# One-bank PSUM tiles throughout, a 384/128 split of the last tile, and newly made orders in a fused attention and GeGLU kernel

## The chip, the cores and the metric

The kernel runs on one NeuronCore of one Trainium2 chip. The metric is the device time in microseconds (us) of one launch. Before the change it is 216.15 us, the median of three runs (215.91 to 216.42).

## What is computed

The input is x, 2048 rows (tokens) of 512 in bf16. It is normalised once, and two branches use the result xn. Branch A is attention over a sliding, dilated window; branch B is a gated feed-forward net. The output is x + A * silu(B).

```python
xn = layernorm(x)
q, k, v = heads(xn @ wqkv)              # 32 heads of 16
# token s looks at s, s-2, ..., s-14 (8 places, those below 0 masked)
logits = einsum("hsd,hswd->hsw", q, k_window) * 16**-0.5
o = einsum("hsw,hswd->hsd", softmax(logits), v_window)
A = o @ wo
h = gelu(xn @ w_gate) * (xn @ w_up)     # 512 -> 1792
B = h @ w_down                          # 1792 -> 512
out = x + A * silu(B)
```

## The kernel before, in words

**Blocks and tiles.** The 2048 tokens are four blocks j = 0 to 3 of 512 tokens, and a block is four tiles tt of 128. For each block TensorE (PE) computes, with matmuls that are nearly all 128x128 by 128x512:

- q, k, v (`qkv`, L527; block 0 tile by tile with 128 columns, L611),
- the gate and up halves of the feed-forward net (`ffn`, L907): 14 chunks fc of each, four matmuls a chunk, named g and u with block and chunk, such as g1_2,
- the down projection (`down`, L971), named y with block, tile, piece and quarter: y0_1_0_2 is block 0, tile 1, piece 0, third quarter. A tile takes 14 matmuls in quarters of 4, 4, 4 and 2,
- the output projection (`out`, L1035), named s: four matmuls a tile.

**Evacuation.** ScalarE (ACT) empties nearly all PSUM tiles: gelu (L923), plain copies of u (L931) and of q, k, v (L542, L544, L549), silu of y (L990), a copy of s (L1050). VectorE (DVE) multiplies gelu and u into h (`geglu`, L945), which the down projection reads. DVE also has the attention: products q*k (L704) and their sums (L716, L720), the softmax, products with v (L850) and their sums.

**The logit sums.** A logit is a sum over 16 products that lie on different partitions. Blocks 1 to 3 form it with accumulating DMAs on GpSimd's queue (`gathered`, L780). Block 0 (`psum=(0,)`) does it on PE (`reduced`): eight matmuls with a matrix of ones (L740) fill a PSUM tile `L0` of two banks; DVE then adds the mask at the sequence's start (L747), takes the maximum over the 8 places (`peak`, L750) and subtracts it (`less`, L757). ACT takes the exponential (L811).

**PSUM.** Eight banks of 128x512 f32 are divided in `POOLS`: pool F has six one-bank tiles, and pool L one tile of two banks. Pool L is for `L0` and, with `shared=True`, for the tiles 0 and 1 of every block's y: `ps_y{j}` of shape [128, 2, 512] holds tile 0 in its first bank and tile 1 in its second. All else goes through F. Dependences are kept by tile: an instruction that writes a tile is made to wait for those that read the same tile earlier in the program's order, whichever bank they read.

**The order of the work.** A planner (`schedule`, L125) walks through all operations with estimated durations, priorities and the list `nudge` of one correction for each operation, and gives one fixed order for each engine and one fixed bank (slot of a pool) for each PSUM tile. The engines then run these orders, each in sequence, with semaphore waits; a waiting instruction holds up all that stands behind it on its engine. The estimates and nudges decide the order only; they are no part of the program.

**The end.** In block 3 the last tile (tt = 3) is split by columns in two pieces at `CUT` = 256, in `down` and in `out`, so that its first piece can be finished and stored while PE still works on the second. The pieces' s is multiplied from PSUM by silu(y) on DVE (gate, L1090), x is added (L1096), and a DMA stores it (L1102); SyncE issues the first piece's store, ACT the second's.

**ACT's tables.** ACT holds one table set at a time. Sqrt (L318), gelu, exp and silu lie in different sets, so each switch inserts a table load; copies need none.

Of the kernel before, what the change touches and what calls it, by code (L numbers as in the profile page):

```python
# [10 lines left out]
ALU = mybir.AluOpType  # L11
AF = mybir.ActivationFunctionType
AX = mybir.AxisListType
BF16 = mybir.dt.bfloat16
F32 = mybir.dt.float32

P = 128
H = 32
DH = 16
W = 8  # L20
# [7 lines left out]
CUT = 256  # L28
# [27 lines left out]
POOLS = {"F": 6, "L": 1, "q": 2, "k": 2, "pr": 5, "attn": 2, "Ls": 1, "v": 2, "o": 1, "oT": 1, "h": 1,  # L56
# [3 lines left out]
    sums=(3,), warm=4, slack=4.68, N=[298.0, 85.4, 406.1, 719.1], psum=(0,), shared=True, rpow=False,  # L60
    S=[238.4, -534.3, 59.4, -251.7], V=[-282.7, -31.0, 282.4, -70.3], Q=[42.0, -337.6, 71.1, 38.0],
    F=[33.6, 79.9, 263.9, 443.0], Y=[-104.4, 20.0, -67.6, -114.6], O=[15.4, -370.2, -327.0, 457.0], vnorm=(),
    vcopy=(1,), vsum=(0,), crowd=1.35,
    nudge=[
# [162 lines left out]
class Kernel:  # L227
# [11 lines left out]
    def new(self, key, shape, dtype, name):  # L239
        pool, slot = self.pool_of[key], self.slot[key]  # L240
        space = self.ps if pool in ("F", "L") else self.sb
        self.t[key] = space.tile(shape, dtype, name=name, tag=f"{pool}{slot}")
        return self.t[key]
# [37 lines left out]
    def layernorm(self, j):  # L281
        base = self.when("N", j)
        for tt in range(TPB):
# [94 lines left out]
            if by_act:  # L378
# [13 lines left out]
                self.op(f"mean{t}", "ACT", 0.62, [f"ld_x{j}_{j}"], mean, prio=prio, slack=(0.0, 0.5, 3.0, 3.0)[j])  # L392
                self.op(f"aggr{t}", "ACT", 0.70, [f"mean{t}"], square, prio=prio)
# [338 lines left out]
    def reduced(self, j):  # L732


        def reduce():
            L = self.new(f"L{j}", [P, 2, TQ], F32, "L_ps")
            for w2 in range(2):
                for tq in range(TPB):
                    pr = self.t[f"pr{j}_{tq // 2}_0"][:, 0, tq % 2, 4 * w2 : 4 * w2 + 4]
                    self.nc.tensor.matmul(  # L740
                        L[H * tq : H * (tq + 1), w2, :], lhsT=self.ind[:],
                        rhs=pr.rearrange("p w t -> p (w t)"), start=True, stop=True,
                    )

        def masked():
            first = self.t["L0"][0:H, :, :].rearrange("p a (b t) -> p (a b) t", b=4)[:, :, 0:PAD]
            self.nc.vector.tensor_tensor(out=first, in0=first, in1=self.mask[:], op=ALU.add)  # L747

        def peak():
            self.nc.vector.tensor_reduce(  # L750
                out=self.peak[:], in_=self.t[f"L{j}"][:].rearrange("p a (b t) -> p t (a b)", b=4),
                axis=AX.X, op=ALU.max,
            )

        def less():
            ls = self.new(f"Ls{j}", [P, W, P], F32, "Ls")
            self.nc.vector.tensor_tensor(  # L757
                out=ls[:], in0=self.t[f"L{j}"][:].rearrange("p a (b t) -> p (a b) t", b=4),
                in1=self.peak[:].unsqueeze(1).to_broadcast([P, W, P]), op=ALU.subtract,
            )  # L760
# [4 lines left out]
        if j == 0:  # L765
            self.op("mask0", "DVE", 0.2, ["red0"], masked, use=["L0"], prio=hot)
# [524 lines left out]
```

## Time and profile before

| what | value |
|---|---|
| median of three runs | 216.15 us |
| the profiled execution: its own time | 215.84 us |
| its span (first to last recorded instruction) | 214.1 us |
| granted TensorE clock | 0.999 of full speed |
| PE, ACT, DVE, GpSimd (POOL) busy | 206.4, 153.1, 187.1, 65.6 us |
| matmul records, ACT table loads | 1105, 19 |

In the rows, the first number is the start in us from the span's start or, in grouped rows, the count after an x. PE is the matmul stream and PEld the loads of weights that run beside it, one for each matmul. A matmul record has a modelled end: a 512-column matmul is shown with 379 ns, though the next starts 0.216 us after it. So the spacing of starts, best read from the weight loads, tells the rate. "[1.45 <-ACT sil L990]" at the end of a row is idle time of the engine before it, and what ended it. In a row of windows the busy time of each engine follows its name.

### The profile page before, as it was taken

To read this page: it belongs to the slowest core of one execution; us is meant where nothing else is said; L and a number is where in the kernel's file an instruction comes from. 1 tells how busy PE (TensorE), PEld (TensorE's weight loads), DVE (VectorE), ACT (ScalarE), POOL (GpSimd) and SP (SyncE) were. 2 spreads that over 40 slices of the span, in tenths; PEclk is the share of its full clock that TensorE was granted. 3 is DMA by queue.
4 is the path that set the end of the run, shared out by engine and by line. 5 is a ranking of instruction groups with operands and counts; after the bars stand their busy time and mean duration, and the time that the engine had idled before them with its cause. 6 is when DMAs were issued, how large, how long until landed. Compare 5 with 4: busy or idle time off the path is not lost.

```text
span 214.1 us, 3070 instructions
## 1 busy us (share of the span) xinstructions
PE 206.4 (96%) x1105; PEld 102.4 (48%) x1123; DVE 187.1 (87%) x211; ACT 153.1 (71%) x258; POOL 65.6 (31%) x108
## 2 busy tenths in 40 slices
PE   7999999999997999999999999999999999999993
PEld 2896444444443444444444544444444444445452
DVE  4698998499899996999999999999999989997114
ACT  3687699999997998767943767877341689665442
POOL 5043200001226679140367740279701010101000
PEclk9999999999999999999999999999999999999999
DMA  5999997205246678762697886168958069506902
GB/s 192 362 382 375 287 278 202 54 0 98 79 117 127 130 135 155 153 167 44 102 168 106 158 212 140 49 116 169 171 99 196 0 132 232 126 2 130 253 13 98
DMA packets 32991, 32.17 MB, mean 150 GB/s; under 512 B 16960, under 2 KB 29520, under 8 KB 32976
## 3 DMA queue, kind: packets, MB, share of 16 engines
q0 software_dynamic: 5136, 14.41, 35.2%
q1 hardware_dynamic: 27008, 16.91, 28.9%
q10 hardware_dynamic: 832, 0.66, 0.9%
q8 instruction: 9, 0.15, 0.3%
q14 instruction: 6, 0.05, 0.1%
HBM read 14.12 MB, written 6.31 MB: 95 GB/s over the span
## 4 chain that ended last, share of the span: by engine, by line
PE 81%; DVE 10%; ACT 6%; issue 2%; ACTq 0%; DVEq 0%
PE u_ps L907 20%; PE y_ps L971 20%; PE g_ps L907 19%; PE qkv_ps L527 14%; PE s_ps L1035 5%; DVE prod L704 4%; PE warm_ps L253 2%; DVE prod L716 2%; PE qkv_ps L611 1%; DVE stats L290 1%; DVE s L1090 1%; DVE s L1096 1%; ACT gl L923 1%; ACT L923 1%; ACT L318 1%
## 5 line engine op out<-in xcount | busy, mean ns | idle before, releaser
L907 PE MATMUL g_ps<-xnT,wg_sb 128*128 128x512 bf16 x219 | 53.5, 379 | 0.3
L971 PE MATMUL y_ps<-wd_sb,hT 128*128 128x512 bf16 (+1 forms) x233 | 51.7, 366 | 2.0 <-ACT sil L990 1.7
L907 PE MATMUL u_ps<-xnT,wu_sb 128*128 128x512 bf16 x221 | 52.9, 379 | 0.2
L780 POOL DMA_DIRECT2D Ls<-prod x48 | 36.4, 887 | 29.0 <-DMA Ls<-prod 10.6
L923 ACT ACTIVATE gl<-g_ps 128x512 bf16<-128x512 f32 x56 | 31.9, 596 | 17.7 <-PE g_ps L907 16.3
L704 DVE TENSOR_TENSOR prod<-q_sb,k_sb 128x2048 bf16<-128x2048 bf16 x32 | 38.0, 1217 | 2.9 <-ACT k_sb L544 1.7
L931 ACT ACTIVATE hT<-u_ps 128x512 bf16<-128x512 f32 x56 | 32.3, 599 | 10.3 <-PE u_ps L907 7.7
L971 PEld LDWEIGHTS <-hT 128*128 128x128 bf16 x238 | 23.3, 98 | 27.5 <-issue 2.4
L850 DVE TENSOR_TENSOR pv<-attn,v_arr 128x4096 bf16<-128x4096 bf16 x16 | 36.2, 2285 | 0.2
L907 PEld LDWEIGHTS <-wu_sb 128*128 128x128 bf16 x224 | 21.9, 98 | 26.4
L907 PEld LDWEIGHTS <-wg_sb 128*128 128x128 bf16 x224 | 21.8, 98 | 26.3 <-issue 0.4
L945 DVE TENSOR_TENSOR hT<-hT,gl 128x1024 bf16<-128x1024 bf16 x28 | 18.8, 681 | 3.1 <-ACT gl L923 2.3
L716 DVE TENSOR_TENSOR prod<-prod 128x2048 bf16<-128x2048 bf16 x16 | 19.1, 1216 | 0.1
L873 POOL DMA_DIRECT2D pv<-pv x4 | 3.5, 886 | 40.1 <-DVE pv L850 40.1
L1035 PE MATMUL s_ps<-wo_sb,oT_sb 128*128 128x512 bf16 (+1 forms) x67 | 15.2, 366 | 0.1
L857 DVE TENSOR_TENSOR pv<-pv 128x2048 bf16<-128x2048 bf16 x12 | 14.4, 1217 | 0.1
L676 POOL DMA_DIRECT2D v_arr<-vT_dram x16 | 10.8, 717 | 11.4 <-DMA vT_dram<-vst 5.9
L990 ACT ACTIVATE sil<-y_ps 128x512 bf16<-128x512 f32 (+1 forms) x17 | 9.1, 575 | 6.6 <-PE y_ps L971 6.6
L1050 ACT ACTIVATE s<-s_ps 128x512 bf16<-128x512 f32 x15 | 9.0, 600 | 5.8 <-PE s_ps L1035 5.6
L569 POOL DMA_DIRECT2D vT_dram<-vst x12 | 7.9, 658 | 15.5 <-ACT vst L549 15.5
L527 PE MATMUL qkv_ps<-xnT,wv_sb 128*128 128x512 bf16 x47 | 11.9, 379 | 0.1
L527 PE MATMUL qkv_ps<-xnT,wk_sb 128*128 128x512 bf16 x48 | 11.8, 379 | 0.0
(93 smaller groups left out, 224.9 us busy)
## 6 DMA issues: line engine op xcount, KB each, us to landing
Ls<-prod POOLq DMA_DIRECT2D x48, 128.0 KB, 3.7
v_arr<-vT_dram POOLq DMA_DIRECT2D x16, 142.0 KB, 4.6
vT_dram<-vst POOLq DMA_DIRECT2D x16, 128.0 KB, 3.5
pv<-pv POOLq DMA_DIRECT2D x4, 512.0 KB, 4.5
oT_dram<-o_sb SPq DMA_DIRECT2D x16, 128.0 KB, 3.3
oT_sb<-oT_dram SPq DMA_DIRECT2D x4, 512.0 KB, 4.3
wg_sb<-in_B_w_gate_dram SPq DMA_DIRECT2D x2, 896.0 KB, 10.1
wu_sb<-in_B_w_up_dram SPq DMA_DIRECT2D x2, 896.0 KB, 12.4
```

What stands on the lines that cost most here:

```text
L527: self.nc.tensor.matmul(ps[:], lhsT=self.w_qkv(which, dk, c), rhs=self.t[f"xT{j}"][:, dk, :], start=(dk == 0), stop=(dk == NC - 1),)
L704: self.nc.vector.tensor_tensor(out=self.t[pair][:, c % 2].rearrange("p n w t -> p w n t"), in0=q.unsqueeze(1).to_broadcast([P, W, 2, P]), ...
L716: self.nc.vector.tensor_tensor(out=pr[:, 0], in0=pr[:, 0], in1=pr[:, 1], op=ALU.add)
L780: self.nc.gpsimd.dma_start(out=self.t[f"Ls{j}"][H * tq : H * (tq + 1)], in_=self.t[f"pr{j}_{tq // 2}_0"][s::NC, 0, tq % 2], **(dict(accum_ ...
L850: self.nc.vector.tensor_tensor(out=pv[:], in0=self.t[f"at{j}"][:, 2 * i : 2 * i + 2, :].unsqueeze(2).to_broadcast([P, 2, DH, P]), in1=win, ...
L857: self.nc.vector.tensor_tensor(out=pv[:, 0], in0=pv[:, 0], in1=pv[:, 1], op=ALU.add)
L907: nc.tensor.matmul(ps[:], lhsT=w[:, dk, fc * P : (fc + 1) * P], rhs=self.t[f"xT{j}"][:, dk, :], start=(dk == 0), stop=(dk == NC - 1),)
L923: self.nc.scalar.activation(out=self.t[f"gl{j}_{pair}"][:, fc % 2, :], in_=self.t[f"ps_g{j}_{fc}"][:], func=AF.Gelu_apprx_tanh,)
L931: self.nc.scalar.activation(out=self.t[f"h{j}"][:, fc, :], in_=self.t[f"ps_u{j}_{fc}"][:], func=AF.Copy)
L945: self.nc.vector.tensor_tensor(out=h, in0=h, in1=self.t[f"gl{j}_{pair}"][:], op=ALU.mult)
L971: nc.tensor.matmul(self.t["ps_" + key][:, 0 : n1 - n0], lhsT=self.t[f"h{j}"][:, fc, tt * P : (tt + 1) * P], rhs=self.wd_sb[:, fc, n0:n1], ...
L1035: self.nc.tensor.matmul(ps[:, 0 : n1 - n0], lhsT=self.t[f"oT{j}"][:, c, tt * P : (tt + 1) * P], rhs=self.wo_sb[:, c, n0:n1], start=(c == 0 ...
```

## The change

1. `POOLS`: pool F has eight one-bank tiles, pool L is gone, and so is `shared`. Each y tile has a bank of its own.
2. `reduced`: block 0's logit sums go into two one-bank tiles of F. What DVE does with them is done in halves: two mask additions, two maxima and one maximum of the two (into a new small tile `peak2`), and two subtractions.
3. `CUT` is 384: the last tile's pieces are 384 and 128 columns wide, in y and in s.
4. Orders: `nudge`, the priorities (N, S, V, Q, F, Y, O), `slack` and the planner's estimates for two ACT operations (`mean`, `aggr`) are other numbers. All engines' orders are new. ACT has 23 table loads where it had 19: one more pair (sqrt, then gelu again) stands early in block 0's feed-forward net, and one more pair (gelu, then silu again) between block 1's silus. Both programs have 2248 PE instructions; those of the kinds above are the same but for the pieces' widths.

```diff
-CUT = 256
+CUT = 384
...
-POOLS = {"F": 6, "L": 1, "q": 2, "k": 2, "pr": 5, "attn": 2, "Ls": 1, "v": 2, "o": 1, "oT": 1, "h": 1,
+POOLS = {"F": 8, "q": 2, "k": 2, "pr": 5, "attn": 2, "Ls": 1, "v": 2, "o": 1, "oT": 1, "h": 1,
...
         def reduce():
-            L = self.new(f"L{j}", [P, 2, TQ], F32, "L_ps")
             for w2 in range(2):
+                L = self.new(f"L{j}_{w2}", [P, TQ], F32, "L_ps")
                 for tq in range(TPB):
...
-        def masked():
-            first = self.t["L0"][0:H, :, :].rearrange("p a (b t) -> p (a b) t", b=4)[:, :, 0:PAD]
-            self.nc.vector.tensor_tensor(out=first, in0=first, in1=self.mask[:], op=ALU.add)
+        def masked(w2):
+            first = view(w2)[0:H, :, 0:PAD]
+            self.nc.vector.tensor_tensor(
+                out=first, in0=first, in1=self.mask[:, half * w2 : half * (w2 + 1), :], op=ALU.add
+            )
...
+        def both():
+            self.nc.vector.tensor_tensor(out=self.peak[:], in0=self.peak[:], in1=self.peak2[:], op=ALU.max)
...
+        for w2 in range(2):
+            before = self.op(f"peak{j}_{w2}", "DVE", 0.66, [before], lambda w2=w2: peak(w2), use=banks, prio=hot)
+        before = self.op(f"peak{j}", "DVE", 0.2, [before], both, prio=hot)
+        for w2 in range(2):
+            before = self.op(f"less{j}" + "a" * (1 - w2), "DVE", 0.62, [before], lambda w2=w2: less(w2),
...
-                        if a == 0 and (tt > 1 or not self.par["shared"]):
-                            self.t["ps_" + key] = self.new("ps_" + key, [P, D], F32, "y_ps")[:]
-                        elif a == 0:
-                            if tt == 0:
-                                self.new(f"ps_y{j}", [P, 2, D], F32, "y_ps")
-                            self.t["ps_" + key] = self.t[f"ps_y{j}"][:, tt, :]
+                        if a == 0:
+                            self.new("ps_" + key, [P, D], F32, "y_ps")
...
-                                 take=[("FL"[both], bank)] if a == 0 and not (both and tt) else [],
+                                 take=[("F", bank)] if a == 0 else [],
```

The new order of PE around the end of block 0's down projection, which the prediction speaks of:

```
before: ... y0_0_0_3 y0_1_0_2 y0_1_0_3 y0_3_0_2 y0_3_0_3 u1_4 k2_3 v2_3 q2_0 v2_1 ...
after:  ... y0_0_0_3 y0_1_0_2 y0_1_0_3 y0_3_0_3 u1_4 u1_0 y0_2_0_3 g1_4 v2_3 v2_1 ...
```

At the end PE's order is now s3_0 s3_2 s3_1, then the last six matmuls of y's 384-column piece and its s3_3_0, then ten matmuls of y's 128-column piece and the four of s3_3_1. Before, it was s3_0 s3_3_0 s3_2 s3_1, then ten matmuls of y's second piece and s3_3_1.

More of the change, by code (lines that the diff above doesn't have):

```diff
@@ L54 @@
 WORK = {"turn": 0.8, "st": 0.42, "ld": 0.82, "sto": 0.6, "ldo": 1.8, "acc": 2.6, "gat": 0.45, "out": 0.8, "end": 0.05}
-POOLS = {"F": 6, "L": 1, "q": 2, "k": 2, "pr": 5, "attn": 2, "Ls": 1, "v": 2, "o": 1, "oT": 1, "h": 1,
+POOLS = {"F": 8, "q": 2, "k": 2, "pr": 5, "attn": 2, "Ls": 1, "v": 2, "o": 1, "oT": 1, "h": 1,
          "xT": 2, "gl": 3, "sil": 1, "s16": 1, "xn": 4, "vst": 4}
 PARAMS = dict(
-    sums=(3,), warm=4, slack=4.68, N=[298.0, 85.4, 406.1, 719.1], psum=(0,), shared=True, rpow=False,
-    S=[238.4, -534.3, 59.4, -251.7], V=[-282.7, -31.0, 282.4, -70.3], Q=[42.0, -337.6, 71.1, 38.0],
-    F=[33.6, 79.9, 263.9, 443.0], Y=[-104.4, 20.0, -67.6, -114.6], O=[15.4, -370.2, -327.0, 457.0], vnorm=(),
+    sums=(3,), warm=4, slack=2.82, N=[306.5, 111.8, 418.2, 728.4], psum=(0,), rpow=False,
+    S=[237.0, -554.0, 60.7, -257.2], V=[-277.9, -35.1, 276.7, -102.3], Q=[43.7, -338.2, 71.3, 36.8],
+    F=[34.7, 79.8, 266.5, 442.4], Y=[-106.0, 20.0, -72.7, -105.7], O=[19.3, -380.8, -324.0, 455.3], vnorm=(),
     vcopy=(1,), vsum=(0,), crowd=1.35,
     nudge=[
[43 rows of a table removed]
[44 rows of a table added]
     ],
@@ L240, in new @@
         pool, slot = self.pool_of[key], self.slot[key]
-        space = self.ps if pool in ("F", "L") else self.sb
+        space = self.ps if pool == "F" else self.sb
         self.t[key] = space.tile(shape, dtype, name=name, tag=f"{pool}{slot}")
@@ L390, in square @@
                     )
-                self.op(f"mean{t}", "ACT", 0.62, [f"ld_x{j}_{j}"], mean, prio=prio, slack=(0.0, 0.5, 3.0, 3.0)[j])
-                self.op(f"aggr{t}", "ACT", 0.70, [f"mean{t}"], square, prio=prio)
+                self.op(f"mean{t}", "ACT", 0.70, [f"ld_x{j}_{j}"], mean, prio=prio, slack=(0.0, 0.5, 3.0, 3.0)[j])
+                self.op(f"aggr{t}", "ACT", 0.75, [f"mean{t}"], square, prio=prio)
             elif t == 1:
@@ L732, in reduced @@
     def reduced(self, j):
+        half = W // 2
         def reduce():
-            L = self.new(f"L{j}", [P, 2, TQ], F32, "L_ps")
             for w2 in range(2):
+                L = self.new(f"L{j}_{w2}", [P, TQ], F32, "L_ps")
                 for tq in range(TPB):
-                    pr = self.t[f"pr{j}_{tq // 2}_0"][:, 0, tq % 2, 4 * w2 : 4 * w2 + 4]
+                    pr = self.t[f"pr{j}_{tq // 2}_0"][:, 0, tq % 2, half * w2 : half * (w2 + 1)]
                     self.nc.tensor.matmul(
-                        L[H * tq : H * (tq + 1), w2, :], lhsT=self.ind[:],
+                        L[H * tq : H * (tq + 1), :], lhsT=self.ind[:],
@@ L742, in reduce, with view @@
                         rhs=pr.rearrange("p w t -> p (w t)"), start=True, stop=True,
                     )
-        def masked():
-            first = self.t["L0"][0:H, :, :].rearrange("p a (b t) -> p (a b) t", b=4)[:, :, 0:PAD]
-            self.nc.vector.tensor_tensor(out=first, in0=first, in1=self.mask[:], op=ALU.add)
-        def peak():
+        def view(w2):
+            return self.t[f"L{j}_{w2}"][:].rearrange("p (w t) -> p w t", w=half)
+        def masked(w2):
[3 more added lines that the diff above has]
+            )
@@ L750, in peak @@
+        def peak(w2):
             self.nc.vector.tensor_reduce(
-                out=self.peak[:], in_=self.t[f"L{j}"][:].rearrange("p a (b t) -> p t (a b)", b=4),
-                axis=AX.X, op=ALU.max,
-            )
-        def less():
-            ls = self.new(f"Ls{j}", [P, W, P], F32, "Ls")
+                out=(self.peak, self.peak2)[w2][:], in_=view(w2).rearrange("p w t -> p t w"), axis=AX.X, op=ALU.max
+            )
+        def both():
+            self.nc.vector.tensor_tensor(out=self.peak[:], in0=self.peak[:], in1=self.peak2[:], op=ALU.max)
@@ L757, in less @@
+        def less(w2):
+            if w2 == 0:
+                self.new(f"Ls{j}", [P, W, P], F32, "Ls")
             self.nc.vector.tensor_tensor(
-                out=ls[:], in0=self.t[f"L{j}"][:].rearrange("p a (b t) -> p (a b) t", b=4),
-                in1=self.peak[:].unsqueeze(1).to_broadcast([P, W, P]), op=ALU.subtract,
+                out=self.t[f"Ls{j}"][:, half * w2 : half * (w2 + 1), :], in0=view(w2),
+                in1=self.peak[:].unsqueeze(1).to_broadcast([P, half, P]), op=ALU.subtract,
@@ L760, in less @@
             )
         hot = -10.0
-        self.op(f"red{j}", "PE", 2 * MM, [f"ladd{j}_0", f"ladd{j}_1"], reduce, mode="tiled", take=[("L", f"L{j}")],
-                use=[f"pr{j}_0_0", f"pr{j}_1_0", f"L{j}"], prio=-100.0, slack=self.par["slack"])
-        if j == 0:
-            self.op("mask0", "DVE", 0.2, ["red0"], masked, use=["L0"], prio=hot)
-        self.op(f"peak{j}", "DVE", 1.24, [f"red{j}" if j else "mask0"], peak, use=[f"L{j}"], prio=hot)
-        self.op(f"less{j}", "DVE", 1.15, [f"peak{j}"], less, take=[("Ls", f"Ls{j}")], use=[f"L{j}", f"Ls{j}"], prio=hot)
+        banks = [f"L{j}_0", f"L{j}_1"]
@@ new lines, in reduced @@
+        self.op(f"red{j}", "PE", 2 * MM, [f"ladd{j}_0", f"ladd{j}_1"], reduce, mode="tiled",
+                take=[("F", b) for b in banks], use=[f"pr{j}_0_0", f"pr{j}_1_0", *banks], prio=-100.0,
+                slack=self.par["slack"])
+        before = f"red{j}"
+        for w2 in range(2):
+            if j == 0:
+                before = self.op(f"mask0_{w2}", "DVE", 0.15, [before], lambda w2=w2: masked(w2), use=banks, prio=hot)
+        for w2 in range(2):
+            before = self.op(f"peak{j}_{w2}", "DVE", 0.66, [before], lambda w2=w2: peak(w2), use=banks, prio=hot)
@@ L770, in gathered @@
+        before = self.op(f"peak{j}", "DVE", 0.2, [before], both, prio=hot)
+        for w2 in range(2):
+            before = self.op(f"less{j}" + "a" * (1 - w2), "DVE", 0.62, [before], lambda w2=w2: less(w2),
+                             take=[("Ls", f"Ls{j}")] if w2 == 0 else [], use=[*banks, f"Ls{j}"], prio=hot)
     def gathered(self, j):
@@ L977, in down @@
                     need = before + [f"geglu{j}_{p}" for p in range(a // 2, b // 2)] + ["ld_wd" + "a" * (b <= 8)]
-                    both = tt < 2 and self.par["shared"]
-                    if both and tt and a == 0:
-                        need.append(f"mm_y{j}_0_0_0")
-                    bank = f"ps_y{j}" if both else "ps_" + key
+                    bank = "ps_" + key
                     nm = self.op(f"mm_{key}_{i}", "PE", (b - a) * MM * (n1 - n0) / D, need, mms,
-                                 take=[("FL"[both], bank)] if a == 0 and not (both and tt) else [],
+                                 take=[("F", bank)] if a == 0 else [],
                                  use=[bank, f"h{j}"], prio=base + 3.05 * tt + 0.9 * i + si, slack=self.par["slack"])
@@ L1226 @@
     k.peak = cpool.tile([P, P], F32, name="peak")
+    k.peak2 = cpool.tile([P, P], F32, name="peak2")
     k.junk = cpool.tile([P, D], BF16, name="junk")
```

87 rows, old and new, of the table nudge are left out of this document.

## The prediction

> **What bounds the kernel now.** I read the page's head and its chain of waits first, then who waited for whom on PE, then the timeline at each wait.
>
> ```profile
> span 214.1 us, 3070 instructions
> PE 206.4 (96%) x1105; PEld 102.4 (48%) x1123; DVE 187.1 (87%) x211; ACT 153.1 (71%) x258; POOL 65.6 (31%) x108
> PE 81%; DVE 10%; ACT 6%; issue 2%; ACTq 0%; DVEq 0%
> PE y_ps L971 <- ACT sil L990: 1.7, 2, 1.5
> ```
>
> PE is busy 96% of the span, and 81% of the chain that ended last is PE. Once it runs, the longest sum of waits on PE is that of the down projection (L971) for silu on ACT, 1.7 us in two waits. So a microsecond that PE loses in mid-kernel is lost to the end, unless something else is late there too. How long PE really stood is read from the weight loads, whose starts show the rate:
>
> ```profile
> 62.24 3.55 PEld L971 LDWEIGHTS <-hT 128*128 128x128 bf16 x17
> 67.52 1.39 PEld L971 LDWEIGHTS <-hT 128*128 128x128 bf16 x7 [1.73 <-issue]
> 62.45 3.62 PE L971 MATMUL y_ps<-wd_sb,hT 128*128 128x512 bf16 x16
> 67.52 1.89 PE L971 MATMUL y_ps<-wd_sb,hT 128*128 128x512 bf16 x8 [1.45 <-ACT sil L990]
> 66.87 0.60 ACT L990 ACTIVATE sil<-y_ps 128x512 bf16<-128x512 f32 x1
> 126.01 2.26 PEld L971 LDWEIGHTS <-hT 128*128 128x128 bf16 x11
> 128.55 1.82 PEld L971 LDWEIGHTS <-hT 128*128 128x128 bf16 x9 [0.29 <-issue]
> 127.90 1.57 ACT L990 ACTIVATE sil<-y_ps 128x512 bf16<-128x512 f32 x3
> 198.06 4.92 PE L971 MATMUL y_ps<-wd_sb,hT 128*128 128x512 bf16 x25
> 202.58 0.60 ACT L990 ACTIVATE sil<-y_ps 128x512 bf16<-128x512 f32 x1 [2.42 <-PE y_ps L971]
> 203.23 2.97 PE L971 MATMUL y_ps<-wd_sb,hT 128*128 128x512 bf16 x14 [0.25 <-ACT sil L990]
> ```
>
> The records of 16 and of 8 matmuls differ by 8: (3.62 - 1.89)/8 = 0.216 a matmul. The 17th weight load belongs to y0_1_0_2, whose matmul was due at 62.24 + 17 x 0.216 = 65.91. It started at 67.52, right after the silu of y0's tile 0 (66.87 + 0.60): **1.61 us lost**. Tiles 0 and 1 share one two-bank tile, so the write of tile 1 waits for the read of tile 0, though they are in different banks. The same meets y1_1 at 128.55, after silu1_0 ended (127.90 + 0.60 = 128.50): due at 126.01 + 11 x 0.216 = 128.39, **0.16 lost**. And y3_1 at 203.23, after silu3_0 (203.18): its record of 25 ends at 202.98 with a 256-column matmul of 0.27, which gives way after 0.11 (both from the rows of the tail, below), so it was due at 202.82: **0.41 lost**. Together 2.18 us.
>
> **The change part by part.**
>
> *One bank for each y tile.* The three waits have no cause left: tile 1 has its own bank, whose last reader was done before its first quarter. Taken off: 2.18 us. What is late next? PE runs 1.6 us ahead of where it was, so it asks for banks sooner, and ACT has to give them. ACT stands thus:
>
> ```profile
> 18.00:66.00 48.00, 47.74 (x223) 21.99 (x227) 42.57 (x54) 45.03 (x80) 6.70 (x11) 1.00 0.58 151
> 34.00:66.00 32.00, 31.84 (x151) 14.71 (x153) 27.33 (x35) 31.29 (x56) 4.09 (x7) 1.00 0.33 72
> 100.00:130.00 30.00, 29.84 (x137) 14.00 (x138) 29.93 (x28) 18.56 (x31) 16.05 (x22) 1.00 0.85 145
> 18.99 0.24 ACT L586 ACTIVATE k_sb<-k_sb 128x64 bf16<-128x64 bf16 x1
> 19.25 1.28 ACT L923 ACT_TABLE_LOAD   x1
> 20.55 1.08 ACT L923 ACTIVATE gl<-g_ps 128x512 bf16<-128x512 f32 x2
> ```
>
> The columns after the length are PE, PEld, DVE, ACT and POOL. From 18 to 66 us ACT idles 48.00 - 45.03 = 2.97 us, but from 34 on only 0.71. The new order does the same 84 ACT operations ahead of silu0_0, and one sqrt/gelu pair of table loads more, early: 2 x 1.28 = 2.56. If the idle time takes it all, silu0_0 ends where it did, at 67.47; if none, at 70.03. In the new order PE does 0.43 less work ahead of y0_1_0_2 (two matmuls), so it gets there at 65.91 - 0.43 = 65.48. The first group that takes the bank of y0_0 is v2_3, with 22 matmuls between (2 + 2 + 4 + 4 + 2 + 4 and the four of y0_1_0_2): 65.48 + 22 x 0.216 = 70.23. So PE finds this bank free with 0.2 to 2.8 us to spare. Then v2_1, at 71.1, takes y0_1's, whose silu stands two operations further (norm15 0.7 and itself 0.6): 68.8 to 71.3. Even at the bad end PE waits about 0.2. I take 0, since the idle time is over the 2.56, and keep up to 2.56 for later groups.
>
> The Trainium skill, page "ScalarE: Activation LUTs", section "What ACT_TABLE_LOAD costs", prices a switch at 1283 ns for the load and about 1380 ns for a drain. The rows show the load but no drain: one ends at 19.23, the load runs from 19.25, and the next activation starts at 20.55. With the drain four more loads would be 10.6 us of ACT, not 5.1; I hold to the rows.
>
> The second pair stands between silu1_0 and silu1_3, where ACT idles 11.4 us of 30 (the row from 100). I take 0 there too.
>
> *Logit sums in two banks.* PE's eight matmuls are the same. DVE's work is cut up:
>
> ```profile
> L747 DVE TENSOR_TENSOR L_ps<-L_ps,mask 32x128 f32<-32x128 f32 x1 | 0.3, 287 | 0.8 <-PE L_ps L740 0.8
> L750 DVE TENSOR_REDUCE peak<-L_ps 128x128 f32<-128x1024 f32 x1 | 1.2, 1226 | 0.0
> L757 DVE TENSOR_TENSOR Ls<-L_ps,peak 128x1024 f32<-128x1024 f32 x1 | 1.2, 1224 | 0.0
> L817 DVE TENSOR_TENSOR tot<-attn 128x512 f32<-128x512 bf16 x4 | 2.7, 687 | 3.7 <-ACT attn L811 3.7
> 38.24 1.22 DVE L757 TENSOR_TENSOR Ls<-L_ps,peak 128x1024 f32<-128x1024 f32 x1
> 40.35 1.28 ACT L811 ACT_TABLE_LOAD   x1
> 41.64 1.06 ACT L811 ACTIVATE attn<-Ls 128x1024 bf16<-128x1024 f32 x1
> 42.73 0.69 DVE L817 TENSOR_TENSOR tot<-attn 128x512 f32<-128x512 bf16 x1 [2.98 <-ACT attn L811]
> ```
>
> No row has the halves. A half of the maximum or the subtraction lies between 0.61 (half) and 1.22 (no saving); the 512-element row gives 0.69, and I take that. The maximum of two works on 128 elements like the mask row, 0.29. A half mask lies between 0.14 and 0.29; I take 0.22. Sum: 2 x 0.22 + 4 x 0.69 + 0.29 = 3.49 for 2.74, so 0.75 more (0.3 to 3.0 more). The cover: the subtraction ended at 39.46, while ACT's exponential came only at 41.64, behind its table load, and DVE then idled 2.98. Up to 2.2 us are free; without that cover it would be 0.75 of DVE, and geglu behind it. I take 0.
>
> *The 128-column piece.* Its matmuls are shown by block 0's rows of that width:
>
> ```profile
> 7.50 0.61 PE L611 MATMUL qkv_ps<-xnT,wk_sb 128*128 128x128 bf16 x8
> 9.07 1.06 PE L611 MATMUL qkv_ps<-xnT,wk_sb 128*128 128x128 bf16 x16
> 209.06 1.25 PE L971 MATMUL y_ps<-wd_sb,hT 128*128 128x256 bf16 x10
> 210.15 0.60 PE L1035 MATMUL s_ps<-wo_sb,oT_sb 128*128 128x256 bf16 x4
> ```
>
> (1.06 - 0.61)/8 = 0.056 each, against 0.054 for a quarter of 0.216; 256 columns take (1.25 - 0.60)/6 = 0.108, and one such record 0.60 - 3 x 0.108 = 0.27. Eighteen matmuls of 128 columns cost 0.04 more; 384 columns, not shown, lie between 0.108 and 0.216, on the line at 0.162. The Trainium skill, "TensorE: Matmul & The Clock Gate", section "Back-to-back issue gap", gives 81 ns for each 128-column matmul in a sustained stream with its weight loads: a rule against narrow pieces, 18 x 25 ns = 0.45 us by it. The rows of 8 and 16 are such a stream and show 56.
>
> *The tail.*
>
> ```profile
> 210.86 0.42 DVE L1090 TENSOR_TENSOR s<-s_ps,sil 128x256 bf16<-128x256 f32 x1
> 211.32 0.29 DVE L1096 TENSOR_TENSOR s<-s,x_sb 128x256 bf16<-128x256 bf16 x1
> 211.64 0.37 ACTq L1102 DMA_DIRECT2D out_dram<-s  x1
> ```
>
> Now PE's last matmul starts at 210.15 + 3 x 0.108 = 210.47, and the last store is issued at 211.64: 1.17 later. After the change, count from the start S of the last 384-column matmul. Fourteen of 128 columns follow, the last at S + 0.16 + 13 x 0.056 = S + 0.89. DVE's gate of the 384 piece starts at S + 0.38 (matmul 0.33, hand-over 0.05) and takes 0.55 (256 columns take 0.42; 0.42 to 0.84), its addition 0.36 (0.29 to 0.58), the gate of 128 columns 0.28 and its addition 0.22 (each from half of the 256 row to all of it). With 0.04 between dependent ones and 0.08 of overlap between the pieces, the store goes out at about S + 1.82, or 0.93 after PE's last start. That last start is 0.05 later against the same total of columns, since the final matmul is the shorter one. Saved: 1.17 - 0.93 - 0.05 = 0.19 (0.4 lost to 0.4 gained). The landing (211.64 to 214.1) I leave.
>
> **The sum**, against the profiled execution's own 215.84 us: -2.18 + 0.04 - 0.19 = -2.33, so 213.5. The median shown, 216.15, is 0.31 higher; I forecast the median: **213.8 us**, with 213.2 to 214.6 for this case by itself.
>
> **The rivals.**
>
> *A true wait takes the place of the false one* (chance 0.12). ACT is full from 34 to 66 us, and the new sqrt/gelu pair comes ahead of that. What its idle time doesn't absorb comes out at 66 to 80 us as waits of PE for banks, 0.5 to 2 us of the 2.18 back. Against it: the margin of 0.2 to 2.8 at v2_3. It gives 214.3 to 215.8; PE would show idle time ended by ACT gelu, u or q/k/v copies.
>
> *The waits were not on the path* (0.03). DVE is full from 100 to 130 in the row above, and all through 130 to 160 us. If DVE sets the pace, an earlier PE gains nothing, and only the tail is left: 216.0.
>
> ```profile
> 130.00:160.00 30.00, 29.84 (x138) 13.61 (x139) 29.80 (x30) 20.22 (x33) 14.80 (x20) 1.00 0.64 120
> L704 DVE TENSOR_TENSOR prod<-q_sb,k_sb 128x2048 bf16<-128x2048 bf16 x32 | 38.0, 1217 | 2.9 <-ACT k_sb L544 1.7
> ```
>
> Against it: DVE itself waited 1.7 us for a k that PE and ACT made, so it moves forward with PE.
>
> *Slower: the attention comes too late for PE* (0.06). In the new DVE order block 1's maximum, which waits for sixteen gathers on GpSimd's queue, stands ahead of a geglu (geglu1_1) that block 1's first y quarter needs; before, that geglu stood ahead of it. If a gather lands late, DVE stands at the maximum with geglu behind it, and PE behind that.
>
> ```profile
> Ls<-prod POOLq DMA_DIRECT2D x48, 128.0 KB, 3.7
> ```
>
> A gather takes 3.7 us, and four follow each other for each quarter, so one round late costs up to 3.7 us; it decides when it outruns PE's stock of other work by more than the 2.33 gained. Full price: 213.8 + 3.7 = 217.5; I place it at 216.6 to 217.5. Before, DVE shows no idle time ended by a gather; that speaks against it.
>
> **How the numbers follow.** Forecast 0.79, true wait 0.12, off the path 0.03, late gathers 0.06. The range 213.1 to 215.2 holds the forecast's own, with the tail's bounds, and most of the first rival; about 0.13 is left out. A change within 0.2% (0.43 us, about what a measurement of this kernel can tell) is the second rival and a sliver of the first: 0.04. Slower by more: 0.06. Faster: 0.90.
>
> **What would show it.** Right: on PE no idle time at L985 (the new number of L971) ended by silu, and PE's last matmul about 2.2 us earlier, at 208.2 to 208.5; the exponential of block 0 no later behind its table load; the last store 0.9 us after PE's last start. Wrong: PE idle after 66 us ended by ACT's copies (first rival), by DVE at hT near 95 to 110 us (third), or by the oT load before the last s tiles.

## The result, and the profile after

The changed kernel takes **213.62 us** (median of four runs, 213.45 to 213.94); the kernel before, in the same set, 216.27 us (215.91 to 216.42). The ratio is 0.9882, with a 95% interval of 0.9864 to 0.9899, or 2.2 to 2.9 us less. The forecast was 213.8 us. The profiled executions, 215.84 and 213.45 us, differ by 2.39.

These lines of the page of after answer to those of before: the span, the engines' busy time, and the shares of the chain that ended last.

```profile
span 211.6 us, 3097 instructions
PE 206.6 (98%) x1123; PEld 101.4 (48%) x1123; DVE 187.3 (88%) x215; ACT 156.5 (74%) x262; POOL 65.7 (31%) x108
PE 94%; DVE 2%; DMA 1%; ACT 1%; issue 0%; SPq 0%
```

PE went from 81% to 94% of the chain. The view of who waited for whom on PE has only entries of the first microseconds left:

```profile
PE warm_ps L254 <- DVE eps L1251: 1.3, 1, 1.3
PE tr_ps L483 <- DVE xn L475: 0.2, 1, 0.2
PE qkv_ps L612 <- ACT xnT L490: 0.2, 1, 0.2
```

The entry of y for silu, 1.7 us before, is gone. The timeline of after shows the place where PE had stood for 1.61 us (L985 is the old L971, L1001 the old L990, L925 the old L907, L528 the old L527):

```profile
62.34 4.05 PE L985 MATMUL y_ps<-wd_sb,hT 128*128 128x512 bf16 x18
66.22 1.89 PE L925 MATMUL u_ps<-xnT,wu_sb 128*128 128x512 bf16 x8
66.76 0.60 ACT L1001 ACTIVATE sil<-y_ps 128x512 bf16<-128x512 f32 x1
69.24 1.89 PE L528 MATMUL qkv_ps<-xnT,wv_sb 128*128 128x512 bf16 x8
```

The 18 matmuls start at 62.34 and the next kind at 66.22, 18 x 0.216 later: no gap. The silu of y0's tile 0 runs as late as before, but PE no longer waits for it. Its bank, free at 67.36, is next written at 69.24, by v2_3.

The end of the program, in the timeline of after:

```profile
206.85 0.81 PE L1046 MATMUL s_ps<-wo_sb,oT_sb 128*128 128x384 bf16 x4
207.50 0.72 PE L985 MATMUL y_ps<-wd_sb,hT 128*128 128x128 bf16 x10
207.77 0.56 DVE L1101 TENSOR_TENSOR s<-s_ps,sil 128x384 bf16<-128x384 f32 x1
208.06 0.39 PE L1046 MATMUL s_ps<-wo_sb,oT_sb 128*128 128x128 bf16 x4
208.26 0.28 ACT L1001 ACTIVATE sil<-y_ps 128x128 bf16<-128x128 f32 x1 [0.72 <-PE y_ps L985]
208.37 0.36 DVE L1107 TENSOR_TENSOR s<-s,x_sb 128x384 bf16<-128x384 bf16 x1
208.64 0.28 DVE L1101 TENSOR_TENSOR s<-s_ps,sil 128x128 bf16<-128x128 f32 x1
208.96 0.22 DVE L1107 TENSOR_TENSOR s<-s,x_sb 128x128 bf16<-128x128 bf16 x1
209.21 0.36 ACTq L1113 DMA_DIRECT2D out_dram<-s  x1
```

PE's last matmul starts at 208.06 + 3 x 0.056 = 208.23, the last store is issued at 209.21, 0.98 later; before it was 1.17. A matmul of 384 columns takes (207.50 - 206.85)/4 = 0.162, one of 128 columns (208.06 - 207.50)/10 = 0.056.

**A ruler.** The first 9 us, called the head here, differ between executions of one and the same kernel: the row used below starts at 8.89 in one of after and at 9.60 in another (the last section says more). So kernels are compared below by one stretch of their profiled executions: from the start of the third row of k weight loads, sixteen in one record, in block 0, to the issue of the last store. These rows are from the timelines of before and of after; before's store, at 211.64, and after's, at 209.21, are shown already.

```profile
9.01 0.95 PEld L611 LDWEIGHTS <-wk_sb 128*128 128x128 bf16 x16
```
```profile
8.89 0.95 PEld L612 LDWEIGHTS <-wk_sb 128*128 128x128 bf16 x16
```

| kernel | k loads | last store | stretch | against before | median us (its runs) | ratio, 95% |
|---|---|---|---|---|---|---|
| before | 9.01 | 211.64 | 202.63 | | 216.1 to 216.3 | |
| after | 8.89 | 209.21 | 200.32 | -2.31 | 213.62 (4) | 0.9882 (0.9864 to 0.9899) |
| after again (e9) | 9.60 | 209.92 | 200.32 | -2.31 | 213.82 (4) | 0.9887 (0.9871 to 0.9903) |
| e1, one bank each | 9.07 | 209.51 | 200.44 | -2.19 | 213.65 (4) | 0.9887 (0.9873 to 0.9900) |
| e2, DVE halves | 9.11 | 211.74 | 202.63 | 0.00 | 216.02 (11) | 0.9995 (0.9985 to 1.0005) |
| e3, two lines exchanged | 9.02 | 210.04 | 201.02 | -1.61 | 214.23 (4) | 0.9912 (0.9898 to 0.9925) |
| e4, after, tied | 9.11 | 209.43 | 200.32 | -2.31 | 213.72 (4) | 0.9888 (0.9874 to 0.9901) |
| e5, after, 256 | 8.85 | 209.29 | 200.44 | -2.19 | 214.27 (5) | 0.9912 (0.9899 to 0.9925) |
| e10, the same again | 9.01 | 209.46 | 200.45 | -2.18 | 214.17 (4) | 0.9906 (0.9892 to 0.9920) |
| e6, after, one pair more | 9.06 | 210.41 | 201.35 | -1.28 | 214.78 (5) | 0.9941 (0.9929 to 0.9953) |
| e7, after, two pairs more | 10.92 | 214.32 | 203.40 | +0.77 | 216.99 (7) | 1.0040 (1.0025 to 1.0055) |
| e8, after, 448 | 8.89 | 209.59 | 200.70 | -1.93 | 214.20 (4) | 0.9912 (0.9899 to 0.9925) |
| e11, one bank each, 384 | 9.51 | 210.33 | 200.82 | -1.81 | 214.35 (9) | 0.9926 (0.9901 to 0.9952) |

Two executions of after agree to 0.01 in the stretch, and so do two of the kernel with pieces of 256 columns; each other kernel has one. In the thirteen profiled executions the head goes from 8.85 to 10.92, while the rest of the time, outside head and stretch, is 4.1 to 4.4 in all. So it is mostly the head that differs from one execution to the next, and medians of a few runs scatter by some 0.3 us with it. By their medians e1 and e3 came out 0.15 and 0.17 below the ranges expected of them, and e5 and e8 0.27 and 0.10 above; by the stretch all four came as expected.

### The profile page after: what moved, and what is told of

Same layout as the page of the kernel before. It is cut to its first block, busy times and chain, and to the rows that moved or that the text cites. A ratio compares the mean times of both kernels' runs of the same rounds, so it can differ in the third digit from the quotient of the medians.

```text
span 211.6 us, 3097 instructions
## 1 busy us (share of the span) xinstructions
PE 206.6 (98%) x1123; PEld 101.4 (48%) x1123; DVE 187.3 (88%) x215; ACT 156.5 (74%) x262; POOL 65.7 (31%) x108
## 4 chain that ended last, share of the span: by engine, by line
PE 94%; DVE 2%; DMA 1%; ACT 1%; issue 0%; SPq 0%
PE g_ps L925 23%; PE u_ps L925 23%; PE y_ps L985 22%; PE qkv_ps L528 15%; PE s_ps L1046 6%; PE qkv_ps L612 5%; DMA x_sb<-in_A_x_dram 1%; DVE s L1101 1%; DVE s L1107 0%; ACT s L1061 0%; ACT xnT L374 0%; PE L_ps L742 0%; PE tr_ps L365 0%; DVE xnT L372 0%; DVE stats L299 0%
## 5 line engine op out<-in xcount | busy, mean ns | idle before, releaser
L925 PE MATMUL g_ps<-xnT,wg_sb 128*128 128x512 bf16 x224 | 54.2, 380 | 0.0
L925 PE MATMUL u_ps<-xnT,wu_sb 128*128 128x512 bf16 x224 | 53.6, 379 | 0.0
L985 PE MATMUL y_ps<-wd_sb,hT 128*128 128x512 bf16 (+2 forms) x238 | 51.8, 367 | 0.0
L798 POOL DMA_DIRECT2D Ls<-prod x48 | 36.9, 872 | 27.2 <-DMA Ls<-prod 12.4
L941 ACT ACTIVATE gl<-g_ps 128x512 bf16<-128x512 f32 x56 | 31.9, 598 | 16.0 <-PE g_ps L925 12.8
L985 PEld LDWEIGHTS <-hT 128*128 128x128 bf16 x238 | 22.7, 98 | 25.9
L925 PEld LDWEIGHTS <-wu_sb 128*128 128x128 bf16 x224 | 21.9, 98 | 26.4
L925 PEld LDWEIGHTS <-wg_sb 128*128 128x128 bf16 x224 | 21.7, 98 | 26.1 <-issue 0.4
L570 POOL DMA_DIRECT2D vT_dram<-vst x12 | 8.9, 745 | 35.5 <-ACT vst L550 35.4
L1046 PE MATMUL s_ps<-wo_sb,oT_sb 128*128 128x512 bf16 (+2 forms) x68 | 15.6, 367 | 0.0
L1001 ACT ACTIVATE sil<-y_ps 128x512 bf16<-128x512 f32 (+2 forms) x17 | 9.3, 574 | 5.3 <-PE y_ps L985 5.2
L1074 POOL DMA_DIRECT2D s<-x_sb x3 | 2.8, 930 | 31.3 <-DVE tot L835 15.7
L528 PE MATMUL qkv_ps<-xnT,wq_sb 128*128 128x512 bf16 x48 | 12.0, 379 | 0.0
```

Of the source, the lines that this page charges most:

```text
L528: self.nc.tensor.matmul(ps[:], lhsT=self.w_qkv(which, dk, c), rhs=self.t[f"xT{j}"][:, dk, :], start=(dk == 0), stop=(dk == NC - 1),)
L798: self.nc.gpsimd.dma_start(out=self.t[f"Ls{j}"][H * tq : H * (tq + 1)], in_=self.t[f"pr{j}_{tq // 2}_0"][s::NC, 0, tq % 2], **(dict(accum_ ...
L925: nc.tensor.matmul(ps[:], lhsT=w[:, dk, fc * P : (fc + 1) * P], rhs=self.t[f"xT{j}"][:, dk, :], start=(dk == 0), stop=(dk == NC - 1),)
L941: self.nc.scalar.activation(out=self.t[f"gl{j}_{pair}"][:, fc % 2, :], in_=self.t[f"ps_g{j}_{fc}"][:], func=AF.Gelu_apprx_tanh,)
L985: nc.tensor.matmul(self.t["ps_" + key][:, 0 : n1 - n0], lhsT=self.t[f"h{j}"][:, fc, tt * P : (tt + 1) * P], rhs=self.wd_sb[:, fc, n0:n1], ...
L1046: self.nc.tensor.matmul(ps[:, 0 : n1 - n0], lhsT=self.t[f"oT{j}"][:, c, tt * P : (tt + 1) * P], rhs=self.wo_sb[:, c, n0:n1], start=(c == 0 ...
```

## The experiments

**Theory:** PE stood three times behind silu because tiles 0 and 1 of y shared one tile for the bookkeeping of dependences (2.18 us); that is gone, and the tail is a little shorter. **Rivals:** the gain comes from the new orders and eight rotating banks; or silu, or ACT, was late for a bank that was really needed.

### e1: one bank each, in before's orders

```diff
...
-                            if tt == 0:
-                                self.new(f"ps_y{j}", [P, 2, D], F32, "y_ps")
-                            self.t["ps_" + key] = self.t[f"ps_y{j}"][:, tt, :]
+                            self.t["ps_" + key] = self.ps.tile([P, D], F32, name="y_ps", tag=f"L{tt}")[:]
...
```

> The kernel before with its own orders and its own banks; only the two-bank tile is two one-bank tiles, for y's tiles 0 and 1 and for block 0's logit sums (whose DVE work is then done in halves). Theory (the three false waits of PE on silu, 1.61 + 0.16 + 0.41 us, were what the change took away): 216.3 - 2.2 = 214.1 us (213.8 to 214.5), and PE has no idle time at the down projection ended by silu. Rival (the new orders and eight rotating banks make the gain): 216.3 us, with waits of PE on other banks where the three were.

Measured 213.65 us; the stretch is 2.19 us shorter. The timeline of e1 on PE and ACT (L981 is down, L1000 silu) has the 24 matmuls of y in one record, where before had 16 and 8 with a hole between; its view of waits on PE has no entry for y either:

```profile
62.52 5.34 PE L981 MATMUL y_ps<-wd_sb,hT 128*128 128x512 bf16 x24
66.94 0.60 ACT L1000 ACTIVATE sil<-y_ps 128x512 bf16<-128x512 f32 x1
```

So the whole 2.18 came from the tiles, without any new order, and with 19 table loads where after has 23. The Trainium skill, page "PSUM — Partial Sum Buffer", section "PSUM bank collisions raise a hardware error", asks to guard PSUM with semaphores by bank and quadrant. A tile over two banks made a coarser guard, and here that difference is the 2.19.

### e2: DVE's halves alone

The two-bank tile stays; the mask, the maximum and the subtraction of block 0's logits are done in halves, as in after.

```diff
...
-                in1=self.peak[:].unsqueeze(1).to_broadcast([P, W, P]), op=ALU.subtract,
+            for w2 in range(2):
+                self.nc.vector.tensor_tensor(
+                    out=ls[:, half * w2 : half * (w2 + 1), :], in0=view(w2),
+                    in1=self.peak[:].unsqueeze(1).to_broadcast([P, half, P]), op=ALU.subtract,
+                )
...
```

> The kernel before with its two-bank tile; only DVE's work on block 0's logit sums is done in halves (two masks, two maxima and one of the two, two subtractions), 0.6 us more by the profile after. Theory (the exponential's table load and ACT's work before it cover this): no change, 216.3 us. Rival (DVE sets the pace there): 0.6 us slower, 216.9 us.

No change. The timeline of e2 on DVE and ACT:

```profile
36.75 0.48 DVE L755 TENSOR_TENSOR L_ps<-L_ps,mask 32x64 f32<-32x64 f32 x2 [0.82 <-PE L_ps L744]
37.27 1.29 DVE L761 TENSOR_REDUCE peak<-L_ps 128x128 f32<-128x512 f32 x2
38.59 0.29 DVE L765 TENSOR_TENSOR peak<-peak,peak 128x128 f32<-128x128 f32 x1
38.91 1.29 DVE L770 TENSOR_TENSOR Ls<-L_ps,peak 128x512 f32<-128x512 f32 x2
41.74 1.06 ACT L824 ACTIVATE attn<-Ls 128x1024 bf16<-128x1024 f32 x1
42.83 0.69 DVE L830 TENSOR_TENSOR tot<-attn 128x512 f32<-128x512 bf16 x1 [2.34 <-ACT attn L824]
```

The halves take 0.48 + 1.29 + 0.29 + 1.29 = 3.35 us, 0.61 more than the 2.74 before. The exponential starts at 41.74, before at 41.64, with the k loads 0.10 later in e2: at the same place. DVE's wait for it shrank from 2.98 to 2.34. The 0.61 was paid out of waiting time.

### e3: two operations exchanged in the program

The two-bank tile stays. The last quarter of y0's tile 1, two matmuls, is written ahead of tile 0's silu; no engine's own order changes.

```diff
+    at = [o.name for o in order]
+    late = order.pop(at.index("mm_y0_1_0_3"))
+    order.insert(at.index("silu0_0_0"), late)
     for o in order:
```

> The kernel before with its two-bank tile and the same order on each engine; in the program, the last quarter of y0's tile 1 (two matmuls) is written ahead of the silu of tile 0 and no longer behind it, so it isn't made to wait for that silu. Theory (the wait comes from the tile's bookkeeping, by the place in the program): the 1.61 us of block 0 go and the 0.57 of blocks 1 and 3 stay: 214.7 us (214.4 to 215.0). Rival (PE waits since silu or ACT is late for a bank that is really needed, or since PE's write and ACT's read in one tile can't run together): 216.3 us.

Measured 214.23 us, and 1.61 in the stretch, to the hundredth the one wait. In the timeline of e3, block 0's record is whole, and the wait of block 1 is still there:

```profile
62.46 5.34 PE L971 MATMUL y_ps<-wd_sb,hT 128*128 128x512 bf16 x24
66.88 0.60 ACT L990 ACTIVATE sil<-y_ps 128x512 bf16<-128x512 f32 x1
126.95 1.82 PEld L971 LDWEIGHTS <-hT 128*128 128x128 bf16 x9 [0.29 <-issue]
```

So neither ACT nor the silu was late for anything: the wait came from where two lines stood in the program. It also shows *which* quarter waited: the one that was moved, y0_1_0_3. In before's program it is the only quarter of that tile behind tile 0's silu.

### e4: the shared tile's dependences put back in after

```diff
...
+                            if tt == 1 and fc == a:
+                                self.wait(i, f"silu{j}")
...
+                    if tt == 0:
+                        self.wait(i, f"y{j}")
+                        self.made[f"silu{j}"] = i
...
```

> The kernel after with its eight banks and its orders; only the dependences that a shared tile would give are put back by hand: a quarter of tile 1 waits for tile 0's silu if it stands behind it in the program, and that silu waits for the quarters of tile 1 ahead of it. Theory in its sharper form (sharing costs only where the program has a quarter of tile 1 shortly behind tile 0's silu; in the new program blocks 0, 2 and 3 have all quarters ahead of it, and block 1's stand 7 us behind): at most 0.2 us slower, 213.6 to 213.8 us. Rival (sharing by itself costs the 2.2 us): 215.8 us, with PE idle behind silu at the down projection.

No loss (213.72 us; the stretch as in after). The new program has no quarter of tile 1 shortly behind tile 0's silu, so these waits cost nothing in it. One bank each takes the 2.18 away in the old program (e1); in the new program the dependences alone would not have brought it back. The new orders with the two-bank tile itself, which leaves six banks for all else, were not run.

### e6 and e7: how much ACT time was left to give

```diff
     for o in order:
+        if o.name in ("gelu0_3",):
+            nc.scalar.activation(out=k.spare[:], in_=k.eps[:], func=AF.Sqrt)
         o.emit()
```

e7 names gelu0_9 as well.

> The kernel after with one more sqrt activation on ACT at about 26 us, ahead of a gelu, so one more pair of table loads: 2.56 us and some 0.25 for the activation, 2.8 in all. Its result is used by nothing. Theory (the change's own extra pair was hidden by ACT's idle time, and there is a little cover left): ACT idles 1.1 us from 18 to 66, so the silu of y0's tile 0 comes 1.7 us late, and the bank that it frees has 1.9 us to spare; only readers before that, whose margins no row gives, can lose something: 213.6 to 214.6 us, likeliest under 214. Rival (idle time is the only cover): 1.7 us slower, 215.3. Rival (ACT is far from the path here): no change, and silu no later.

> As the kernel with one more pair of table loads, and a second one at about 50 us: 5.6 us more of ACT ahead of block 0's silus. Theory (cover is 1.1 us of idle time and 1.9 of margin at the bank): 2.6 us slower than after, 216.2 us (215.2 to 217.0), with PE idle behind ACT. Rival (idle time is the only cover): 4.5 us slower, 218.1. Rival (ACT is far from the path): 213.6.

e6 took 214.78 us, above the range expected, and lost 1.03 us of stretch against after. The loss isn't where the theory looked. The timeline of e6 on ACT, DVE and PE (L319 is the square root, L767 the subtraction, L985 down, L941 gelu):

```profile
38.82 1.28 ACT L319 ACT_TABLE_LOAD   x1
40.12 0.30 ACT L319 ACTIVATE rstd<-mv,eps 128x4 f32<-128x4 f32 x1
40.45 0.18 DVE L325 RECIPROCAL rstd<-rstd 128x4 f32<-128x4 f32 x1 [1.28 <-ACT rstd L319]
41.19 0.68 DVE L767 TENSOR_TENSOR Ls<-L_ps,peak 128x512 f32<-128x512 f32 x1
41.93 1.04 PE L985 MATMUL y_ps<-wd_sb,hT 128*128 128x512 bf16 x4 [0.84 <-DVE Ls L767]
```

and the same operations in after:

```profile
37.54 0.30 ACT L319 ACTIVATE rstd<-mv,eps 128x4 f32<-128x4 f32 x1
38.62 0.69 DVE L767 TENSOR_TENSOR Ls<-L_ps,peak 128x512 f32<-128x512 f32 x1
40.75 1.03 PE L985 MATMUL y_ps<-wd_sb,hT 128*128 128x512 bf16 x4
```

Read along the semaphores: ACT's square root for block 2's norm comes 2.41 late (40.12 - 37.54, less the 0.17 by which the k loads differ). DVE has its reciprocal in front of the subtraction of the logits, and stands. The subtraction ends at 41.87, and only then is the bank of the logits' second half free, which the first quarter of y0's tile 0 takes. In after that quarter had 40.75 - 39.31 = 1.44 us from the subtraction's end, some 1.4 to spare; 2.4 late is 1.0 lost. In e7 the second pair stops PE once more, for another bank, which waits for a gelu behind the reload:

```profile
55.02 1.03 PE L528 MATMUL qkv_ps<-xnT,wv_sb 128*128 128x512 bf16 x4
56.00 1.28 ACT L941 ACT_TABLE_LOAD   x1
57.95 0.81 PE L528 MATMUL qkv_ps<-xnT,wq_sb 128*128 128x512 bf16 x3 [1.90 <-ACT gl L941]
```

Due at 55.02 + 4 x 0.216 = 55.88, it started 2.07 late. Together 1.0 + 2.07 = 3.1, and the stretch is 3.08 longer than after's. e7's 216.99 us is at the upper end of its range (2.6 us lost were expected), and a third of the loss came by DVE and not straight from ACT. So of ACT's 2.8 us of one more pair, 0.4 went into idle time, 1.4 into that margin, and 1.0 to the end.

### e5, e8 to e11: the cut and the end of the order

e5 and e10 are after with `CUT = 256`, e8 with `CUT = 448`, e11 is e1 with `CUT = 384`, all with their orders and banks held as they were; e9 is after once more.

```diff
...
+    first, order = plan(src=src)
+    CUT = 256
+    k, same = plan(src=src)
+    k.slot = first.slot
+    by = {o.name: o for o in same}
+    order = [by[o.name] for o in order]
...
```

> The kernel after with its orders and banks; only the last tile's pieces are 256 and 256 columns again. Theory (the cut at 384 is worth the tail's 0.19 less the 0.04 of narrow matmuls): 0.15 us slower than after, 213.8 us (213.6 to 214.0), with 1.17 us from PE's last start to the last store where after has 0.98. Rival (the tail is the larger part of what the waits don't explain): 0.4 us or more slower, 214.1.

> The kernel after with its orders and banks; only the last tile's pieces are 448 and 64 columns. By the rows (a 64-column matmul between 0.028 and 0.056 us, the first piece's matmuls 0.027 longer each, the gate and addition of 448 columns some 0.1 longer than of 384): the last matmul of the wide piece starts 0.35 to 0.46 us later and the last store goes out about as long after it as before, so 0.3 to 0.5 us slower than after, 213.9 to 214.1. Rival (the narrower the last piece the better): 0.1 to 0.2 faster, 213.4 to 213.5.

> The kernel after once more, beside the same with the cut at 256 columns on one chip, since their medians of different sets stand 0.65 us apart but their profiles only 0.1. If the cut is worth 0.1 us, both come out within 0.3 us of each other; if it is worth 0.6, this one is at 213.6 and the other at 214.2.

> The kernel after with pieces of 256 and 256 columns again, beside the kernel after on one chip. By the rows 0.1 to 0.15 us slower than it; by the medians of the separate sets 0.65.

> The kernel before with its own orders, the two-bank tile as two one-bank tiles, and the last tile's pieces 384 and 128 columns: the whole change but for the new orders, with 19 table loads where after has 23. If the orders add nothing, the time of after, 213.5 us (213.3 to 213.9), and by the profile 2.3 us less than before from block 0's k matmuls to the last store, as after has. If the new orders were needed for the tail, it stays at the 2.2 us of the split alone.

The medians of e5 and after, from different sets, suggest 0.65 us for the cut; side by side (e9, e10) they differ by 0.35, a little over the 0.3 expected, with overlapping intervals, and the stretch says 0.12 and 0.13. At 448 columns it is 0.38 worse than at 384, as the rows had it. **e11 missed its expectation**: by the stretch it is 0.38 *slower* than e1, not 0.12 faster. Its timeline on PE and DVE:

```profile
208.68 0.39 PE L1045 MATMUL s_ps<-wo_sb,oT_sb 128*128 128x128 bf16 x4
208.95 0.42 DVE L1100 TENSOR_TENSOR s<-s,sil 128x512 bf16<-128x512 bf16 x1
209.41 0.42 DVE L1106 TENSOR_TENSOR s<-s,x_sb 128x512 bf16<-128x512 bf16 x1
209.75 0.28 DVE L1100 TENSOR_TENSOR s<-s_ps,sil 128x128 bf16<-128x128 f32 x1
210.33 0.37 ACTq L1112 DMA_DIRECT2D out_dram<-s  x1
```

In before's order a whole tile's s (s3_1) comes just ahead of the last, now shorter piece of PE's work, and its gate and addition of 512 columns are still on DVE when the last piece is ready: the store goes out 1.48 after PE's last start. The new order, which puts all whole tiles ahead of the pieces, is what lets the narrow cut gain.

## Why the prediction was right, step by step

- **The three waits, 2.18 us.** Right: 2.19 in e1. The size came from the spacing of weight loads; block 0's alone is 1.61 in e3, which leaves 0.58 for the other two, where 0.57 was forecast.
- **Which quarter waited.** Wrong: the prediction says y0_1_0_2, and it was y0_1_0_3 (e3). After the hole stood 8 matmuls, 2 + 4 + 2, which fits only that one. The size of the wait didn't hang on the name. So the way to v2_3 was 18 matmuls and not 22: 65.48 + 18 x 0.216 = 69.37, and v2_3 started at 69.24, with the k loads 0.12 earlier. The margin came out at 1.9 us, inside the 0.2 to 2.8.
- **Four more table loads at nothing.** Right: e1, with before's orders and 19 loads, and e5, with the new orders and 23, have the same stretch, so loads and orders together cost nothing. The silu ended at 67.36, at the early end of 67.47 to 70.03 when the 0.12 is added. But the step that looked for the margin only at v2_3 and v2_1 looked in the wrong place: less was to spare at the y quarter at 40.75, through DVE and the logits' bank, with 1.4 us. That this wasn't overrun was in part luck: the prediction had not looked there, and one more pair would have cost 1.0 (e6). The first rival, a true wait, was nearer than its argument let it seem.
- **DVE's halves.** Right at 0: 0.61 us more instead of the 0.75 forecast, within waiting time (e2).
- **The tail.** Right within its bounds: 0.98 from PE's last start to the last store (0.93 forecast, 1.17 before). The 0.05 more is the start of DVE's gate, 207.77 - (206.85 + 3 x 0.162) = 0.43 after the last 384-column matmul's start, where 0.38 was forecast. Matmuls of 128 columns took 0.056, so the 0.45 us that the prediction gave as the other price of narrow ones didn't come. The cut's net in the stretch is 0.12 to 0.13 (0.15 forecast), in the new orders alone: in before's it is a loss of 0.38 (e11). The last store landed 2.39 after its issue, at the span's end, and 2.46 before; this 0.07, which the prediction left out, is within the span's rounding.
- **The sum.** Forecast 2.33 against the profiled execution, measured 2.39; in the stretch 2.18 + 0.15 forecast, 2.31 measured. That the median fell by 2.65, some 0.3 more than the stretch, lies within the interval's 2.2 to 2.9 and within the scatter of the head.
- **Rivals.** DVE didn't set the pace: PE moved and the end with it. No gather held PE up; no idle time of PE after 35 us is left. That the new orders alone would have removed the waits, which e4 makes likely, was no rival of the prediction and should have been one.

## What to carry to other kernels

When an engine waits for a reader of a tile, look whether it needs *that* memory: a tile over two banks, or a line that stands behind another in the program, makes waits that no data asks for, and exchanging two lines shows it in one run. When work is added to an engine beside the path, follow every consumer of its results, through the in-order queues of other engines too; here the nearest margin was not at the bank that the delayed operation itself frees. Compare kernels that differ by tenths of a microsecond between two fixed instructions of the trace, not by medians that carry the head.

## What was not expected of the hardware

**The clock at the start.** In the profiled executions of e7 and e11, PE was still slow after its warm-up. The weight loads on e7's timeline:

```profile
6.19 1.59 PEld L612 LDWEIGHTS <-wq_sb 128*128 128x128 bf16 x15 [0.38 <-issue]
7.75 0.89 PEld L612 LDWEIGHTS <-wk_sb 128*128 128x128 bf16 x8
8.60 0.47 PEld L365 LDWEIGHTS <-xn 128*128 128x128 bf16 x4
```

and the same on after's:

```profile
5.82 0.89 PEld L612 LDWEIGHTS <-wq_sb 128*128 128x128 bf16 x15 [0.32 <-issue]
6.66 0.51 PEld L612 LDWEIGHTS <-wk_sb 128*128 128x128 bf16 x8
7.10 0.27 PEld L365 LDWEIGHTS <-xn 128*128 128x128 bf16 x4
```

Eight loads and matmuls take 8.60 - 7.75 = 0.85, or 0.106 each; in after 0.44, or 0.055. From the first of these rows to the sixteen k loads e7 needs 10.92 - 6.19 = 4.73 and after 8.89 - 5.82 = 3.07: 1.66 us lost, while the page's row of the granted clock shows full speed in every slice:

```profile
PEclk9999999999999999999999999999999999999999
```

The Trainium skill, "TensorE: Matmul & The Clock Gate", section "Wait — 56ns, not 53.3ns?", gives 106.7 ns for 128 columns cold and 55.6 warm. The trace agrees with both, so e7's PE ran cold until about 10 us; in e11 only the row of 15 q loads was slow, 1.54 us. Its section "What's actually happening" has the clock follow activity in a window that runs freely, so that the change comes at another time in each run. The times here fit that, but no run here varied the warm-up to test the rule. The clock isn't all of the head's spread: in e9, with no slow row, the transposes of xn already start at 5.76, where after has 5.06, and the sixteen k loads come as much later.

**Narrow matmuls.** In e8, ten matmuls of 64 columns:

```profile
207.88 0.46 PE L985 MATMUL y_ps<-wd_sb,hT 128*128 128x64 bf16 x10
208.17 0.28 PE L1046 MATMUL s_ps<-wo_sb,oT_sb 128*128 128x64 bf16 x4
```

They take (208.17 - 207.88) / 10 = 0.029 us each, with their weight loads, nearly an eighth of 0.216. Down to 64 columns, in this run, the time went by the width.
